# Seven shared PSUM banks with a cap per kind, two by-product tiles for the row maxima, transposes issued four in a run, and another plan

## The chip, the cores and the metric

The kernel runs on one core of a Trainium2 chip. The metric is the device time of one execution in microseconds (us); less is better. PE is the matrix engine (PEld its weight loads), DVE, ACT and POOL are the vector, scalar and general engines, SP issues most DMAs.

## What is computed

Two layers, each an attention block A and a feed-forward block B, on 2048 rows of 512 values, in float32:

```python
x = x + A(layernorm(x)); x = x + B(layernorm(x))      # twice, same weights
# A: 32 heads of 16, four segments of 512 rows, in order
logits = qs @ ks.T * scale + mask
a_dot = softmax(logits) @ vs
a_mem = (phi(qs) @ M) / (phi(qs) @ z + 1e-6)          # memory of the earlier segments
o = g * a_mem + (1 - g) * a_dot
M += phi(ks).T @ vs;  z += sum(phi(ks))
# B, with F = 1792
(silu(x @ w_gate) * (x @ w_up)) @ w_down
```

The mask takes away the keys that lie after the query.

## The kernel before

Precision. A float32 operand is split into a rounded part and a rest (two `float32r` halves); a product is three matmuls (high by high, low by high, high by low). `mm3` (L293), `qk_proj` (L469), `up` (L771) and `down` (L793) do this with 512-column matmuls. Some work stays in plain float32: the transposes by the identity (`ln_transpose` L378, `fin` L555, `post` L640, `mem_update` L677), the product of probabilities and values (`pv` L609), and the reading and updating of the memory (L657, L677). The text calls the first kind split matmuls and the second f32 matmuls.

Units. A unit `u` is 4 heads of one segment: 64 units in all, 8 to a segment (PER), 32 to a layer. For each unit:
- `mx_units` (L528) fills PSUM with the logits, queries on the partitions, 12 tiles of up to 512 columns (16 matmuls of 256, 256, 384 and 512 columns per head). DVE takes the row maximum of each piece (L548), writing the masked logits to a tile `junk` that nobody reads and the maximum to `mx`. `fin` transposes the maxima (L557), ACT negates them and sends them by DMA into a row of `cq`, the unit's query tile.
- `at_units` (L567) computes the logits again, keys on the partitions (L589), now with the maximum subtracted by that row; ACT takes the exponential (L595), POOL clears the masked triangle (L603), `pv` multiplies by the values (L618), and `post` normalises (DVE).

Around the units lie the projections (L290), the memory update (`mem_update`: four transposes of phi(k), an ACT copy, 16 small matmuls), and the feed-forward block of segment `j` (`ffn_items` L750), whose split matmuls are spread over the units of the segment after. In the first 8 to 10 units there is no feed-forward work to put between the attention's; after the last unit there is only feed-forward work left.

What sets the order. Nothing is ordered by hand. Every instruction is recorded as an `Op` with a cost, a priority and its buffers; `Program.issue` (L147) then plays the engines forward by a list of costs (LAT, DRAIN, TABLE and the costs at each `pe`, `act`, `dve`, `gp`), and takes at each moment, on the engine that is free first, the ready instruction with the lowest priority number. That order is written out, each engine runs its own in order, and semaphores keep the data right. The priority is the unit's number plus an offset from the tables ALONE, MIXED, EARLY, FFN and PRE. A change of these numbers moves instructions, not work.

PSUM. Of the 8 banks, `pj` has three that the planner hands out as they come free (projections, feed-forward, most transposes). `pmx` has two in a fixed alternation (row maxima), `plt` two in a fixed alternation (logits for the exponential), `ppv` one. A tile can be written only when the reader of the tile before it in the same bank is done.

Of the kernel before, what the change touches and what calls it, by code (L numbers as in the profile page):

```python
# [27 lines left out]
WOT = ("pmx_0", "pmx_1", "pj", "pj")  # L28
ALONE = {'at': (0.488, 0.659), 'lf': (-1.156, -0.458), 'mr': (1.485, 0.781), 'mu': (0.526, -0.286), 'qk': (-0.342, 0.72), 'v': (-0.297, -0.631), 'lp': (0.497, 0.642), 'mx': (-0.73, 0.16)}
MIXED = {'at': (0.319, 0.977), 'lf': (-0.896, 0.182), 'mr': (0.757, 0.781), 'mu': (0.246, 0.122), 'wo': (0.094, 1.841), 'qk': (-0.29, 0.416), 'v': (0.109, 0.348), 'lp': (0.111, 0.187), 'mx': (0.776, 0.745)}  # L30
EARLY = {'v': 1.068, 'qk': 0.531, 'o': 0.6}
FFN = {'ln': 2.081, 'up': 2.482, 'step': 1.143, 'second': 0.743, 'down': 0.177, 'gu': -0.061, 'd': 0.014}
LEAD = 1.0
PRE = {'c': -1.92, 'mb': 0.123, 'gate': -0.719, 'v': -1.763, 'dv': 0.124, 'qk1': -1.331, 'mx': -1.0}
NP = NF
TABLE = 1.28
TABLE_PRIO = 0.15
DRAIN = {("full", "cols"): 0.195, ("cols", "full"): 0.095}
# [3 lines left out]
    pe=dict(pe=0.01, act=0.35, dve=0.35, sp=0.34),  # L42
    act=dict(act=0.22, dve=0.28, pe=0.42, pool=0.35, sp=0.3),
    dve=dict(dve=0.13, act=0.28, pe=0.4, pool=0.31, sp=0.27),
    pool=dict(pool=0.1, dve=0.21, pe=0.28, act=0.25, sp=0.2),
    sp=dict(act=1.35, dve=1.35, pe=1.35, pool=1.35, sp=1.2),
)


class Buf:  # L50
    def __init__(self, prog, pool, tag, shape, dtype):
# [24 lines left out]
class Program:  # L76
# [70 lines left out]
    def issue(self):  # L147
# [16 lines left out]
        held = {tag: [] for tag in self.shared}  # L164
        for o in self.ops:
            if o.wait == 0:
                heapq.heappush(fut[o.eng], (o.ready, o.index, o))
        done, bus, table, mode = 0, 0.0, "exp", "full"
        while done < len(self.ops):
            best = None  # L170
            for e in engs:
                f, n = fut[e], now[e]
                while True:
# [31 lines left out]
            o = n[0][2]  # L205
            if e == "act" and o.table and o.table != table:
# [31 lines left out]
            for b in o.bufs:  # L238
                b.left -= 1
                if b.left == 0 and b.slot is not None:  # L240
                    free[b.tag].append((end + 0.25, b.slot))
                    for w in held[b.tag]:
                        w.ready = max(w.ready, end + 0.25)
# [10 lines left out]
def infini_swiglu(ctx: ExitStack, tc: tile.TileContext, x, wq, wk, wv, wo, beta, wg, wu, wd, out,  # L254
# [8 lines left out]
    P = Program({"pj": 3})  # L263
# [5 lines left out]
    def bank(tag, ring=1):  # L269
        return P.buf(psum, tag, [128, 512], F32, ring)  # L270

    def pe(n, passes, fn, reads, writes, loads=1, mode="full"):
        o = op("pe", max(passes * n / 2400 + 0.0025 + 0.0145 * loads * (passes == 1), 0.11 * loads), fn, reads, writes)
        o.mode = mode
        return o
# [4 lines left out]
    def dve(n, fn, reads, writes, fast=1):  # L280
        op("dve", n / 960 / fast + 0.0687, fn, reads, writes)
# [77 lines left out]
    def ln_norm(xt, view, xk, tags, on_act=False):  # L359
# [4 lines left out]
        gp(0.46, lambda: nc.gpsimd.tensor_tensor(out=rs.ap[:, 0:1], in0=mv.ap[:, 1:2], in1=mhalf.ap, op=OP.pow),  # L364
# [13 lines left out]
    def ln_transpose(xn, xh, xl, t, tag="pj"):  # L378
        ps = bank(tag)
        for kc in range(KC):  # L380
            pe(128, 2, lambda kc=kc: nc.tensor.transpose(ps.ap[:, kc * 128:(kc + 1) * 128],  # L381
                                                         xn.ap[:, kc * 128:(kc + 1) * 128], ident.ap),
               [xn, ident], [(ps, kc)])
# [5 lines left out]
    def split(raw, rv, hi, hk, hv, lo, lk, lv, on_pool=False):  # L389
        act(512, lambda: nc.scalar.copy(hv(hi.ap), rv(raw.ap)), [raw], [(hi, hk)], sbuf=True)  # L390
        if on_pool:
            gp(1.31, lambda: nc.gpsimd.tensor_sub(lv(lo.ap), rv(raw.ap), hv(hi.ap).bitcast(F32)),  # L392
# [76 lines left out]
    def qk_proj(G, n, nm, tag="pj", nt="nat", rt="raw"):  # L469
# [12 lines left out]
        gp(0.62, lambda: nc.gpsimd.tensor_scalar(out=nat.ap[:, 0, :], in0=raw.ap, scalar1=1.0, scalar2=0.0,  # L482
# [456 lines left out]
```

## Time and profile before

| | |
|---|---|
| time, median of 3 runs (lowest, highest) | 1980.16 us (1979.6, 1980.47) |
| the profiled execution's own time | 1978.77 us |
| its span, first to last instruction | 1977.0 us |
| mean granted PE clock | 0.995 |
| PE busy, PEld busy | 1922.9 us (97%), 1488.2 us (75%) |
| ACT busy, POOL busy | 1171.0 us (59%), 997.2 us (50%) |

A matmul's record runs from its start to a modelled end that lies well after the start of the next, so that records overlap. Idle time of PE in the profile is therefore less than the time lost: a stretch in which the next matmul starts late shows as busy until the record before it ends. The distance between starts is what counts.

### The profile page before, as it was taken

What the parts mean: (1) busy time and instruction counts of PE and PEld (TensorE: products, weight loads), DVE (VectorE), ACT (ScalarE), POOL (GpSimd) and SP (SyncE); (2) the same over time, 40 slices, a digit from 0 to 9 for tenths busy, and PEclk for the clock granted to TensorE, in tenths of its full rate; (3) what the DMA queues carried; (4) which work ended last, traced back from release to release, by engine and by line L of the source; (5) the groups of instructions that cost most, each with busy time, mean ns of one, the idle gap of its engine ahead of it and who ended that gap; (6) DMA issues with size and microseconds to landing.
All of it is one profiled execution on the core that took longest, in us unless ns stands there. A gap on an engine that the chain in (4) does not pass through costs nothing.

```text
span 1977.0 us, 33401 instructions
## 1 busy us (share of the span) xinstructions
PE 1922.9 (97%) x11136; PEld 1488.2 (75%) x11136; DVE 1173.9 (59%) x3376; ACT 1171.0 (59%) x2268; POOL 997.2 (50%) x1139
## 2 busy tenths in 40 slices
PE   7998999999999999999999999999999999999998
PEld 5675777777777777777777787777777777777786
DVE  4775664656656565555645675555755557654454
ACT  3565576656666566655766756666565665664332
POOL 6455555465554555454654655546554464445100
PEclk9999999999999999999999999999999999999999
DMA  7544544456434554444644546434554355333332
GB/s 223 162 134 139 152 120 120 113 142 190 128 107 118 145 182 134 118 123 145 183 138 120 134 145 169 137 101 140 150 159 129 97 155 159 109 87 113 110 96 75
DMA packets 250490, 266.98 MB, mean 135 GB/s; under 512 B 17872, under 2 KB 166352, under 8 KB 250320
## 3 DMA queue, kind: packets, MB, share of 16 engines
q1 hardware_dynamic: 248272, 264.33, 46.3%
q8 instruction: 89, 1.46, 0.3%
q10 hardware_dynamic: 2048, 0.53, 0.1%
q14 instruction: 81, 0.66, 0.1%
HBM read 197.15 MB, written 67.11 MB: 134 GB/s over the span
## 4 chain that ended last, share of the span: by engine, by line
PE 85%; DVE 6%; issue 3%; DMA 3%; ACT 2%; POOL 1%; SPq 0%; DVEq 0%; ACTq 0%; POOLq 0%
PE pj L779 28%; PE pj L290 16%; PE pj L802 13%; PE pmx L541 8%; PE plt L589 7%; PE ppv L618 7%; DVE junk L548 2%; PE pmx L802 2%; PE pj L665 1%; PE pj L381 1%; DMA ck<-scrk 1%; ACT p L595 0%; DVE r L630 0%; PE pj L557 0%; PE pj L681 0%
## 5 line engine op out<-in xcount | busy, mean ns | idle before, releaser
L548 DVE CUSTOM_DVE_ANT_0 junk<-pmx,amask 128x128 bf16<-128x128 f32 (+3 forms) x1024 | 497.6, 486 | 252.0 <-PE pmx L541 200.6
L779 PE MATMUL pj<-fh,gu 128*128 128x512 f32 x1568 | 524.7, 399 | 1.3 <-ACT sg L786 0.7
L595 ACT ACTIVATE p<-plt 128x512 f32<-128x512 f32 (+2 forms) x768 | 334.8, 458 | 175.7 <-PE plt L589 148.5
L802 PE MATMUL pj<-d,h 128*128 128x512 f32 x1176 | 361.6, 399 | 5.8 <-DVE fl L386 1.6
L392 POOL TENSOR_TENSOR gu<-rw,gu 128x512 fp32r<-128x512 f32 x196 | 257.3, 1315 | 208.4 <-ACT gu L390 191.2
L779 PEld LDWEIGHTS pj<-fh,gu 128*128 128x128 f32 x1568 | 289.2, 188 | 55.5 <-ACT sg L786 1.4
L541 PE MATMUL pmx<-ck,cq 127*128 127x256 f32 x992 | 287.6, 337 | 14.5 <-DVE mx L548 10.1
L779 PE MATMUL pj<-fl,gu 128*128 128x512 f32 x784 | 301.5, 401 | 0.0
L589 PE MATMUL plt<-cq,ck 128*128 128x512 f32 x992 | 283.8, 333 | 4.3 <-ACT p L595 2.3
L802 PEld LDWEIGHTS pj<-d,h 128*128 128x128 f32 x1176 | 217.3, 188 | 58.1 <-DVE fl L386 2.3
L541 PEld LDWEIGHTS pmx<-ck,cq 127*128 127x128 f32 x992 | 180.4, 190 | 64.2 <-DVE mx L548 14.5
L589 PEld LDWEIGHTS plt<-cq,ck 128*128 128x128 f32 x992 | 182.8, 190 | 39.2 <-ACT p L595 8.6
L390 ACT CAST gu<-rw 128x512 fp32r<-128x512 f32 x226 | 139.3, 620 | 121.8 <-PE pj L779 64.2
L603 POOL TENSOR_SCALAR_AFFINE_SELECT p<-p 128x512 f32<-128x512 f32 x192 | 124.5, 648 | 170.8 <-ACT p L595 170.0
L805 DVE TENSOR_TENSOR fx<-fx,pj 128x512 f32<-128x512 f32 x196 | 133.1, 682 | 93.0 <-PE pj L802 92.2
L779 PEld LDWEIGHTS pj<-fl,gu 128*128 128x128 f32 x784 | 147.2, 188 | 29.3 <-issue 1.0
L392 POOL TENSOR_TENSOR d<-rw,d 128x512 fp32r<-128x512 f32 x98 | 125.8, 1301 | 61.4 <-ACT d L390 36.8
L787 DVE TENSOR_TENSOR sg<-sg,pj 128x512 f32<-128x512 f32 x112 | 76.6, 684 | 99.5 <-PE pj L779 59.3
L618 PE MATMUL ppv<-p,vt 128*32 128x512 f32 (+2 forms) x1536 | 135.2, 454 | 0.0
L628 DVE STREAM_TRANSPOSE tt<-ppv 128x512 f32<-128x512 f32 x64 | 45.8, 716 | 117.8 <-PE ppv L618 117.7
L786 ACT ACT_TABLE_LOAD x87 | 111.6, 1283 | 2.8 <-PE pj L779 1.3
L790 DVE TENSOR_TENSOR h<-sg,h 128x512 fp32r<-128x512 f32 x112 | 94.6, 845 | 27.7 <-ACT h L789 27.2
(165 smaller groups left out, 3218.3 us busy)
## 6 DMA issues: line engine op xcount, KB each, us to landing
rw<-in_B_w_gate_dram SPq DMA_DIRECT2D x112, 256.0 KB, 3.1
rw<-in_B_w_down_dram SPq DMA_DIRECT2D x112, 256.0 KB, 2.7
rw<-in_B_w_up_dram SPq DMA_DIRECT2D x112, 256.0 KB, 3.0
cq<-scrq SPq DMA_DIRECT2D x124, 192.0 KB, 3.2
ck<-scrk SPq DMA_DIRECT2D x124, 192.0 KB, 4.3
scrq<-nat SPq DMA_DIRECT2D x31, 512.0 KB, 2.8
scrk<-nat SPq DMA_DIRECT2D x30, 512.0 KB, 2.7
rw<-in_A_wv_dram SPq DMA_DIRECT2D x32, 256.0 KB, 2.8
```

Source lines behind the costliest of these rows:

```text
L290: pe(n, passes, lambda: nc.tensor.matmul(view(ps.ap), lhsT=av(a.ap), rhs=bv(b.ap), start=start, stop=stop), [(a, rk[0]), (b, rk[1])], [ps])
L390: act(512, lambda: nc.scalar.copy(hv(hi.ap), rv(raw.ap)), [raw], [(hi, hk)], sbuf=True)
L392: gp(1.31, lambda: nc.gpsimd.tensor_sub(lv(lo.ap), rv(raw.ap), hv(hi.ap).bitcast(F32)), [raw, (hi, hk)], [(lo, lk)])
L541: nc.tensor.matmul(ps.ap[:, a * 256:a * 256 + nk], lhsT=cq.ap[0:127, 2 * j + p, qt * 128:(qt + 1) * 128], rhs=ck.ap[0:127, p, 0:nk], start ...
L548: dve(w, lambda a=a, qt=qt, w=w, ps=ps, junk=junk: nc.vector.tensor_tensor_reduce(out=junk.ap[:, :w], in0=ps.ap[:, a * 256:a * 256 + w], i ...
L589: nc.tensor.matmul(ps.ap[:, c0:c0 + n_], lhsT=ck.ap[:, p, k0:k0 + 128], rhs=cq.ap[:, 2 * j + p, 512 - n_:512], start=True, stop=True)
L595: act(w, lambda Pb=Pb, o0=o0, w=w, i0=i0: nc.scalar.activation(Pb.ap[:, idx, o0:o0 + w], ps.ap[:, i0:i0 + w], AF.Exp, scale=SCALE), [ps], ...
L603: gp(0.593, lambda: nc.gpsimd.affine_select(out=v(), in_=v(), pattern=[[0, 4], [1, 128]], compare_op=OP.is_ge, fill=0.0, base=0, channel_m ...
L618: nc.tensor.matmul(ps.ap[32 * i:32 * i + 32, q0:q0 + w], lhsT=vt.ap[:, kt, VW * hd:VW * hd + 32], rhs=f_[sl].ap[:, idx, c0:c0 + w], start= ...
L779: pe(512, 1, lambda x=x, y=y, kc=kc, z=z, ps=ps, wt=wt: nc.tensor.matmul(ps.ap, lhsT=wt.ap[:, x, kc], rhs=T[y].ap[:, :, kc], start=(z == 0 ...
L802: pe(512, 1, lambda x=x, y=y, z=z, ps=ps, ht=ht, wt=wt, cs=cs: nc.tensor.matmul(ps.ap, lhsT=ht.ap[:, y, cs], rhs=wt.ap[:, x, :], start=(z ...
L805: dve(512, lambda ps=ps, t=t: nc.vector.tensor_add(X.ap[:, t, :], X.ap[:, t, :], ps.ap), [ps, (X, t)], [(X, t)])
```

## The change

- PSUM. `pj`, `pmx` and `plt` become one set of seven banks, `ps`, given out as they come free; `ppv` stays. At most 3 of the seven may hold row-maximum tiles, 3 logits, 4 the rest (CAP).
- Transposes. The four transposes of a tile (layer norm, phi(k), memory) and the two matmuls that fill one bank of a memory read are recorded as one operation, so that nothing comes between them. All f32 matmuls are marked as one mode; where the planner would change the mode, it first takes ready work of the mode it is in, up to 0.572 units later in priority (MODE_PRIO). For activation tables the like allowance goes from 0.15 to 2.787.
- `junk` has two tiles in turn, `nm` one in place of two.
- The planner's costs and latencies, and all tables of offsets, have other values. The units' early table holds two units longer, and the third copy of the query and key tiles one unit longer.

No arithmetic is added or left out; the number of matmuls, reductions, exponentials and splits is the same (a few instructions change engine).

```diff
-WOT = ("pmx_0", "pmx_1", "pj", "pj")
-ALONE = {'at': (0.488, 0.659), 'lf': (-1.156, -0.458), ...
+WOT = ("pmx", "pmx", "pj", "pj")
+ALONE = {'wo': (-0.72, 3.126), 'at': (-2.429, -2.271), ...
-FFN = {'ln': 2.081, 'up': 2.482, 'step': 1.143, 'second': 0.743, 'down': 0.177, 'gu': -0.061, 'd': 0.014}
+FFN = {'ln': 1.126, 'up': 2.673, 'step': 1.087, 'second': 0.857, 'down': 0.247, 'gu': -0.315, 'd': 2.454}
-TABLE_PRIO = 0.15
-DRAIN = {("full", "cols"): 0.195, ("cols", "full"): 0.095}
+TABLE_PRIO = 2.787
+DRAIN = {("full", "f32"): 0.09, ("f32", "full"): 0.0}
+MODE_PRIO = 0.572
+CAP = {"pmx": 3, "plt": 3, "pj": 4}
+SLACK = 0.103
...
-                            if not free[b.tag]:
+                            if not free[b.tag] or used[b.kind] >= CAP[b.kind]:
...
+            if e == "pe" and o.mode != mode:
+                stay = [x for x in n if x[2].mode == mode and x[0] < o.prio + MODE_PRIO
+                        and (x[2].need is None or x[2].need.slot is not None
+                             or (used[x[2].need.kind] < CAP[x[2].need.kind]
+                                 and any(y[0] <= start + 1e-9 for y in free[x[2].need.tag])))]
+                if stay:
+                    x = min(stay)
...
-    P = Program({"pj": 3})
+    P = Program({"ps": 7})
...
-        for kc in range(KC):
-            pe(128, 2, lambda kc=kc: nc.tensor.transpose(ps.ap[:, kc * 128:(kc + 1) * 128],
-                                                         xn.ap[:, kc * 128:(kc + 1) * 128], ident.ap),
-               [xn, ident], [(ps, kc)])
+        def turn():
+            for kc in range(KC):
+                nc.tensor.transpose(ps.ap[:, kc * 128:(kc + 1) * 128], xn.ap[:, kc * 128:(kc + 1) * 128], ident.ap)
+        pe(512, 2, turn, [xn, ident], [ps], mode="f32", cost=0.435)
...
-                    ps = bank("pmx", ring=2)
+                    ps = bank("pmx")
-                        junk = sb("junk", [128, 512], BF16)
+                        junk = sb("junk", [128, 512], BF16, ring=2)
...
-                ps = bank(f"pmx_{t % 2}") if end else bank("pj")
+                ps = bank("pmx" if end and t % 2 else "pj")
```

Three places in the order of PE's instructions. The numbers behind a name are its bank or copy and the buffer. Line numbers differ between the two kernels: L541/L563 fills row-maximum tiles, L557/L579 is the transpose of the maxima, L290/L312 a projection, L681/L709 the transposes of phi(k), L720 the memory update, L618/L640 `pv`, L802/L829 `down`.

First place: PE, early, the row-maximum tiles at the end of unit 0 and the start of unit 1. Before:

```order
L541 MATMUL pmx_0_544<-ck0_99,cq0_67 128x512
L541 MATMUL pmx_1_553<-ck0_99,cq0_67 128x256 x2
L541 MATMUL pmx_0_562<-ck0_99,cq0_67 128x384
L541 MATMUL pmx_1_570<-ck0_99,cq0_67 128x512
L541 MATMUL pmx_0_575<-ck1_215,cq1_204 128x256 x2
L541 MATMUL pmx_1_583<-ck1_215,cq1_204 128x384
L557 MATMUL pj_2_587<-ident_65,mx_0_483 16x128
```

and now:

```order
L563 MATMUL ps_1_538<-ck0_99,cq0_67 128x512
L312 MATMUL ps_5_513<-xl_186,wq_354 128x512 x2
L563 MATMUL ps_2_550<-ck0_99,cq0_67 128x256 x2
L563 MATMUL ps_3_562<-ck0_99,cq0_67 128x384
L563 MATMUL ps_4_565<-ck0_99,cq0_67 128x512
L563 MATMUL ps_6_577<-ck1_234,cq1_212 128x256 x2
L579 MATMUL ps_0_580<-ident_65,mx_0_450 16x128
```

Before, six tiles in a row go to two banks in turn, so that every tile waits for the reader of the tile two ahead of it; now each goes to another bank.

Second place: PE, in the middle of the program (second layer, its first segment), the transposes of phi(k) around a `pv`. Before:

```order
L618 MATMUL ppv_11909<-p1_11789,vt0_82 32x128 x4
L802 MATMUL pj_0_11892<-d_1_11588,h_0_11695 128x512
L802 MATMUL pj_2_11906<-d_1_11588,h_0_11695 128x512
L681 MATMUL pj_1_11936<-ident_65,phik_0_10566 128x128
L802 MATMUL pj_2_11906<-d_0_11581,h_2_11515 128x512
L681 MATMUL pj_1_11936<-ident_65,phik_0_10566 128x128
L802 MATMUL pj_2_11906<-d_1_11588,h_0_11695 128x512
L681 MATMUL pj_1_11936<-ident_65,phik_0_10566 128x128
L802 MATMUL pj_2_11906<-d_0_11581,h_2_11515 128x512
L681 MATMUL pj_1_11936<-ident_65,phik_0_10566 128x128
```

and now:

```order
L579 MATMUL ps_1_11916<-ident_65,mx_1_11631 16x128
L709 MATMUL ps_0_11918<-ident_65,phik_0_10801 128x128 x4
L640 MATMUL ppv_11927<-p0_11661,vt0_82 32x512 x4
L640 MATMUL ppv_11927<-p1_11706,vt0_82 32x384 x4
L640 MATMUL ppv_11927<-pc_11758,vt0_82 32x256 x4
L640 MATMUL ppv_11927<-p1_11706,vt0_82 32x128 x4
L720 MATMUL ps_3_11949<-vt0_82,of_11945 32x34 x16
```

The four transposes stood one by one between split matmuls; now they stand together, and with the transpose of the maxima, `pv` and the memory update make one run of f32 matmuls.

Third place: PE, near the last of the program, `down` of the last feed-forward block. Before:

```order
L802 MATMUL pmx_1_22092<-d_0_22074,h_2_22045 128x512
L802 MATMUL pmx_0_22086<-d_1_22079,h_0_22101 128x512
L802 MATMUL pmx_1_22092<-d_1_22079,h_0_22101 128x512
L802 MATMUL pmx_0_22117<-d_0_22074,h_2_22045 128x512
L802 MATMUL pmx_0_22117<-d_1_22079,h_0_22101 128x512
```

and now:

```order
L829 MATMUL ps_1_22102<-d_0_22067,h_2_22041 128x512
L829 MATMUL ps_2_22100<-d_1_22073,h_0_22097 128x512
L829 MATMUL ps_1_22102<-d_1_22073,h_0_22097 128x512
L829 MATMUL ps_3_22114<-d_0_22067,h_2_22041 128x512
L829 MATMUL ps_6_22117<-d_0_22067,h_2_22041 128x512
```

The third result tile went to the bank of the first (`pmx_0`), one matmul after that was complete; now it goes to another bank.

Counted over all of PE's rows: the 9632 matmuls are the same in both. Stretches of f32 matmuls with no split matmul between them are 385 before and 119 now. On ACT, loads of an activation table are 174 before and 152 now.

More of the change, by code (lines that the diff above doesn't have):

```diff
@@ L267, in sb, with bank, pe @@
         return P.buf(pool, tag, shape, dtype, ring)
[L269 to L273, printed above, removed]
+    def bank(kind):
+        if kind == "ppv":
+            return P.buf(psum, kind, [128, 512], F32)
+        return Buf(P, psum, "ps", [128, 512], F32, kind)
+    def pe(n, passes, fn, reads, writes, loads=1, mode="full", cost=None):
+        o = op("pe", cost or max(n / 2400 + 0.018 * loads, 0.109 * loads), fn, reads, writes)
         o.mode = mode
@@ L581, in f @@
                         f_[sl] = sb("pc", [128, 4, 256])
-                ps = bank("plt", ring=2)
+                ps = bank("plt")
                 need = [(cq, j), (cq, "m"), (ck, 0), (ck, 1)]
@@ L620, in go @@
                                          rhs=f_[sl].ap[:, idx, c0:c0 + w], start=(x == 0), stop=(x == 3))
-            pe(1280, 4, go, [(vt, e) for e in range(8)] + [f_[0], f_[1], f_[2]], [ps], mode="cols")
+            pe(1280, 4, go, [(vt, e) for e in range(8)] + [f_[0], f_[1], f_[2]], [ps], mode="f32", cost=2.29)
         def post():
@@ L640, in post, with turn @@
                     m, tp = g["mem"], bank("pj")
-                    for t in range(4):
-                        o = pe(128, 2, lambda t=t: nc.tensor.transpose(tp.ap[:, t * 128:(t + 1) * 128],
-                                                                       m.ap[:, t], ident.ap), [m, ident], [(tp, t)])
-                        o.deps |= set(f_["pv"].ops[:1])
+                    def turn():
+                        for t in range(4):
+                            nc.tensor.transpose(tp.ap[:, t * 128:(t + 1) * 128], m.ap[:, t], ident.ap)
+                    pe(512, 2, turn, [m, ident], [tp], mode="f32", cost=0.435).deps |= set(f_["pv"].ops[:1])
                 dve(512, lambda: nc.vector.transpose(of.ap, Y.ap.rearrange("p a b -> p (a b)")), [Y], [of])
@@ L679, in mem_update, with turn @@
         vt, ps, phi = VT[G % 2], bank("pj"), g["phik"]
-        for t in range(4):
-            pe(128, 2, lambda t=t: nc.tensor.transpose(ps.ap[:, t * 128:(t + 1) * 128],
-                                                       phi.ap[:, t * 128:(t + 1) * 128], ident.ap),
-               [phi, ident], [(ps, t)])
+        def turn():
+            for t in range(4):
+                nc.tensor.transpose(ps.ap[:, t * 128:(t + 1) * 128], phi.ap[:, t * 128:(t + 1) * 128], ident.ap)
+        pe(512, 2, turn, [phi, ident], [ps], mode="f32", cost=0.435)
         pk = sb("of", [128, 512])
@@ L694, in go @@
                                      rhs=vt.ap[:, t, hd:hd + 2 * VW], start=(t == 0), stop=(t == 3))
-        pe(2 * VW * 4, 4, go, [pk] + [(vt, c) for c in range(8)], [pm], loads=3, mode="cols")
+        pe(2 * VW * 4, 4, go, [pk] + [(vt, c) for c in range(8)], [pm], mode="f32", cost=0.39)
         tmp, m = sb("mtmp", [128, 2, VW]), Mb[n]
@@ L833, in infini_swiglu @@
     for t in range(4):
-        ln_fin(0, t, ("pmx_0", "pmx_1", "pj", "ppv")[t])
+        ln_fin(0, t, ("pmx", "pmx", "pj", "ppv")[t])
     XTL = xT[0][0]
```

72 lines of the change are left out of this document (42 added, 30 removed).

## The prediction, made before the run

> **What bounds the kernel.** I read the engines' shares first, then four stretches of the program, then PE's waits, then single stretches of PE.
>
> ```profile
> span 1977.0 us, 33401 instructions
> PE 1922.9 (97%) x11136; PEld 1488.2 (75%) x11136; DVE 1173.9 (59%) x3376; ACT 1171.0 (59%) x2268; POOL 997.2 (50%) x1139
> PE 85%; DVE 6%; issue 3%; DMA 3%; ACT 2%; POOL 1%; SPq 0%; DVEq 0%; ACTq 0%; POOLq 0%
> ...
> 0.00:25.00 25.00, 12.52 (x48) 10.31 (x49) 14.20 (x46) 12.11 (x21) 16.18 (x35) 0.93 0.57 179
> 25.00:200.00 175.00, 160.71 (x1066) 112.63 (x1065) 112.79 (x399) 96.19 (x233) 96.60 (x120) 0.96 0.55 162
> 200.00:1850.00 1650.00, 1629.83 (x9518) 1270.30 (x9517) 981.31 (x2833) 1024.40 (x1949) 884.43 (x985) 1.00 0.47 135
> 1850.00:1977.00 127.00, 119.82 (x509) 94.92 (x508) 65.60 (x99) 38.33 (x66) 0.00 (x0) 0.99 0.31 92
> ```
>
> (The stretches' columns: length, busy time of PE, PEld, DVE, ACT, POOL, granted PE clock, DMA share, GB/s.) PE is the bound. The change neither adds nor removes a matmul, so it can win only what PE loses between them. Idle is 12.5 us before 25, 14.3 to 200, 20.2 to 1850, 7.2 at the end: 54 us. The loss is larger, because a record outlives its turn:
>
> ```profile
> 703.23 2.48 PE L802 MATMUL pj<-d,h 128*128 128x512 f32 x10
> ```
>
> Ten 512-column matmuls, each of a 0.40 us record, take 2.48, so one starts every (2.48 - 0.40) / 9 = 0.231 us, and a late start hides its first 0.17 us behind the record before it. How this looks early on:
>
> ```profile
> 59.03 0.94 PE L541 MATMUL pmx<-ck,cq 127*128 127x256 f32 x3
> 59.39 0.08 DVE L548 DVE_READ_ACCUMULATOR2_ANT mx<- 128x1 f32 x1
> 59.52 0.19 PEld L541 LDWEIGHTS pmx<-ck,cq 127*128 127x128 f32 x1 [0.30 <-DVE mx L548]
> 60.30 0.08 DVE L548 DVE_READ_ACCUMULATOR2_ANT mx<- 128x1 f32 x1
> 60.53 0.47 PE L541 MATMUL pmx<-ck,cq 127*128 127x512 f32 x1 [0.56 <-DVE mx L548]
> ...
> PEld pmx L541 <- DVE mx L548: 8.8, 21, 0.8
> PEld plt L589 <- ACT p L595: 6.2, 14, 0.9
> PE pmx L541 <- DVE mx L548: 7.1, 16, 1.3
> ```
>
> Four fills stand one behind the other, and from 59.03 to 60.53 PE does what needs about 0.6 us; each fill starts as DVE finishes the tile two ahead. The three waits are those of 25 to 200 (total, times, longest). So the early loss is for two banks, not for an engine: DVE is busy 113 of those 175 us.
>
> **The banks.** The first place in the order shows six fills on two banks; now seven banks take turns. I priced every PE row (0.231 us for 512 columns, by width below that, f32 matmuls by their own rows) and summed PE's work between a tile's last matmul and the first of the next tile in its bank. What a bank needs in between: 0.17 for the last record's end, the reader, and about 0.07 for the signal (DVE ends at 59.47, the load starts at 59.52; elsewhere up to 0.15). The readers:
>
> ```profile
> L548 DVE CUSTOM_DVE_ANT_0 junk<-pmx,amask 128x512 bf16<-128x512 f32 x256 | 175.5, 686 | 81.6 <-PE pmx L541 71.4
> L548 DVE CUSTOM_DVE_ANT_0 junk<-pmx,amask 128x256 bf16<-128x256 f32 x256 | 107.4, 420 | 6.3 <-DVE mx L548 0.2
> L548 DVE DVE_READ_ACCUMULATOR2_ANT mx<- 128x1 f32 x1024 | 84.1, 82 | 0.2
> L548 DVE CUSTOM_DVE_ANT_0 junk<-pmx,amask 128x128 bf16<-128x128 f32 x256 | 73.0, 285 | 110.4 <-PE pmx L541 96.9
> L595 ACT ACTIVATE p<-plt 128x512 f32<-128x512 f32 x256 | 147.1, 600 | 78.8 <-PE plt L589 62.2 <-PE ppv L618 15.5
> ```
>
> A row-maximum tile needs 0.17 + 0.686 + 0.082 + 0.07 = 1.0 us at 512 columns and 1.1 for the pair of small pieces; logits need 0.84. In the first 190 us of PE work (some 230 us of time) 87 of 359 reuses come after less than 1.0 us of work before, and 7 of 369 now. The shortfalls add to 24.7 us before and 1.2 now; in all the rest to 8.6 before and nothing now. So the waits for banks cost about 33 us, and can give between 0 (if the reader's queue, not the bank, is the limit) and 33. I take 18 early and 5 later, **23**, nearer the upper end: 72% and 58% of the shortfall, since PE packed closer meets the other engines sooner.
>
> **The clock.** Within the early stretch the granted clock falls where PE idles:
>
> ```profile
> 50.00:75.00 25.00, 20.96 (x88) 14.91 (x92) 19.62 (x75) 11.72 (x29) 15.42 (x16) 0.93 0.45 144
> 150.00:175.00 25.00, 21.35 (x154) 12.87 (x154) 12.66 (x38) 16.44 (x39) 14.93 (x20) 0.86 0.44 124
> ```
>
> The stretch of 25 to 200 has 0.96: 0.04 x 175 = 7 us of full clock lost; the two quoted pieces are 1.75 and 3.5 of it. Their idle time should shrink with the bank waits. Between 0 and 7 I take **4**. The Trainium skill ("TensorE: Matmul & The Clock Gate", section "A second HAM failure mode: psum-queue depth-cycling") says that short idles of PE between groups that cycle through banks make the clock gate swing; by that rule the whole 7 would come back. Here 75 to 150 has a clock of 1.00 with bank waits in it, which speaks against the whole.
>
> **Transposes in a run, f32 matmuls in a run.** The second place in the order, in the trace of before:
>
> ```profile
> 700.42 0.60 PE L381 MATMUL pj<-ident,xn 128*128 128x128 f32 x4
> ...
> 1015.09 1.32 PE L802 MATMUL pj<-d,h 128*128 128x512 f32 x5
> 1016.34 1.71 PE L618 MATMUL ppv<-p,vt 128*32 128x512 f32 x16
> 1018.30 0.40 PE L618 MATMUL ppv<-p,vt 128*32 128x128 f32 x8
> 1018.63 0.74 PE L802 MATMUL pj<-d,h 128*128 128x512 f32 x2
> 1019.21 0.27 PE L681 MATMUL pj<-ident,phik 128*128 128x128 f32 x1
> 1019.56 0.27 PE L681 MATMUL pj<-ident,phik 128*128 128x128 f32 x1
> 1020.59 0.40 PE L290 MATMUL pj<-wvh,xh 128*128 128x512 f32 x1
> ```
>
> Four transposes with a split matmul behind each take 1020.59 - 1019.21 = 1.38 us; four split matmuls are 0.92, so a transpose alone costs 0.114. In a run it costs (0.60 - 0.27) / 3 = 0.109. So four in a run save 0.02 us a tile: **nothing**. `pv` is another matter: it starts 0.33 us after the last of the five before it (0.10 over 0.231), and the second matmul behind it 0.34 after the first (0.11 over): some 0.2 us to go there and back. A neighbour that joins it can save up to 0.1. Of 64 `pv`, 40 stood alone and 6 do now, and of 24 memory updates 21 and 4: 51 joins at most, between 0 and 5 us; I take **4**. If every one of the 266 stretches that vanish saved 0.09, it would be 24; the rows above say no for a transpose.
>
> **What costs or gives nothing.** Loads of an activation table, 174 to 152, at
>
> ```profile
> L786 ACT ACT_TABLE_LOAD x87 | 111.6, 1283 | 2.8 <-PE pj L779 1.3
> L548 DVEq EVENT_SEMAPHORE  x630: 21/21/21, 43.3 to 1776.6; - x158
> ```
>
> 1.28 us are 28 us of ACT, which is busy 59%; they hide beside PE, and without that cover only those ahead of a wait of PE would count. The second `junk` drops a wait of DVE on itself, at most 630 x 0.021 = 13 us of DVE, hidden likewise but for the early row maxima, where it is in the 18. One `nm` for two: its next use is a unit away (20 us), far beyond the DMA that reads it.
>
> **Both ends.**
>
> ```profile
> 9.05 1.97 PE L381 MATMUL pmx<-ident,xn 128*128 128x128 f32 x8 [9.05 <-ACT xn L370]
> ...
> 1966.98 2.59 PE L802 MATMUL pmx<-d,h 128*128 128x512 f32 x10 [1.50 <-ACT h L789]
> 1970.11 3.03 PE L802 MATMUL pmx<-d,h 128*128 128x512 f32 x12 [0.54 <-DVE p L805]
> ```
>
> At the start SP now sends the rows of x ahead of a piece of `wv`, whose issue took the first 0.4 us, and ACT no longer casts that piece between: about 1 us. At the end, by the third place in the order, the wait of 0.54 (0.7 between starts) goes, that of 1.50 for `h` stays, and the last two additions now come due 0.23 us apart in place of 0.7, so that the second waits 0.4 more. Together I take **2**, between -1 and 4.
>
> **New waits.** The planner now counts about 0.27 us from ACT or DVE to PE (0.17 or 0.16 plus SLACK), 0.42 and 0.40 before, so it places matmuls sooner behind what they need. A weight tile `gu` is loaded, cast by ACT and completed by POOL before PE may use it; of 223 reuses of its three copies 1 lay under 3 us of PE work before, 13 do now. The row of PE's waits that shows it before:
>
> ```profile
> PE pj L779 <- ACT gu L390: 0.9, 1, 0.9
> ```
>
> One wait in the whole program. I take **-1**, nearest to that row; the bound is the second rival. Behind such a matmul everything on PE queues.
>
> **The sum.** 23 + 4 + 4 + 2 - 1 = 32 us off the profiled execution's own 1978.8 (span 1977.0 and 1.8 around it), which lies 1.4 below the median: 1946.8 there, **1948** against the median.
>
> **The rivals.**
> - DVE and ACT take the banks' place: PE early waits for row maxima and exponentials, whatever bank they sit in. For it: DVE's row maxima of a unit are 16 x (0.486 + 0.082), some 9 us, as long as PE's own attention work for it; against it: DVE's 113 of 175. Half the bank and clock terms are left, 13 of 27: 1962.
> - Weights late, **slower**: ACT serves `gu` behind exponentials, since its offset moved from -0.061 to -0.315 (later). The price is a wait at each of 224 pieces; at 0.2 us it is 45, which gives 1993. It decides from 33 / 224 = 0.15 us a piece. Against it: one wait in the row above, and 204 of the reuses leave over 4 us for a cast of 0.6 and a subtraction of 1.3.
> - A stretch of f32 matmuls costs 0.09 to leave and the joins bring 24 in place of 4: 1928.
> - The change does not do what it says: caps of 3 and 3 with 4 others on 7 banks only move the waits to the other kinds: 1978.
> - Long runs of transposes lose the clock. The first 25 us hold a run of 16 transposes at a clock of 0.93, 1.75 us lost; some twelve stretches now hold 12 or more transposes: 12 x 1.75 = 21, which gives 1969. The Trainium skill (the same page, section "Part 4: PE-mode transpose") says that transposes do not count as activity for the gate. From 200 to 1850 the clock reads 1.00 with 35 runs of four in the program, so the trace gives no sign of it.
>
> **Chances.** The forecast 0.62 (its own range 1932 to 1960), DVE and ACT 0.17, the joins 0.06, no effect 0.04, late weights 0.07, the clock 0.04. A measurement of this kernel can tell some 0.2%, 4 us. Faster: 0.62 + 0.17 + 0.06 + 0.04 = 0.89; same 0.04; slower 0.07. The range takes in the whole shortfall and half the joins (33 + 7 + 12 + 4 = 56 off) at its lower end, and at the upper a fifth of the bank term and nothing from clock and joins (5 + 2 - 1 = 6 off): 1924 to 1974.
>
> **What would show it.** Right: from 25 to 200 PE's waits for DVE `mx` and ACT `p` fall from 22 us to under 8, DVE is busier there, the clock reads 0.98 or more; 200 to 1850 gets shorter by some 10; a run of four transposes still costs 0.109 each. Wrong: a new large row of PE waiting for ACT `gu`, or for `lt`'s row of maxima; a `pv` whose surroundings got no cheaper; an early stretch as long as before.

## The result and the profile after

| | before | changed |
|---|---|---|
| time, median (lowest to highest) | 1980.32 us (1979.6 to 1984.02) | 1923.14 us (1921.63 to 1923.6) |
| the profiled execution's own time, its span | 1978.77, 1977.0 us | 1923.43, 1921.7 us |

The ratio is 0.9706, with a 95% interval of 0.9689 to 0.9723: 57 us less, where 32 were forecast. The time lies 0.9 us under the low end of the range. The page of the changed kernel (engines, then the shares of the chain that ended last) and its four stretches, cut as in the prediction:

```profile
span 1921.7 us, 33511 instructions
PE 1883.9 (98%) x11136; PEld 1497.5 (78%) x11136; DVE 1158.1 (60%) x3376; ACT 1134.6 (59%) x2246; POOL 998.1 (52%) x1139
PE 91%; DVE 4%; DMA 2%; issue 1%; ACT 1%; POOL 1%; SPq 0%; DVEq 0%; POOLq 0%; ACTq 0%
...
0.00:25.00 25.00, 15.51 (x66) 12.56 (x67) 16.60 (x49) 13.54 (x23) 17.89 (x38) 1.00 0.57 184
25.00:200.00 175.00, 160.45 (x1177) 121.97 (x1176) 121.50 (x452) 98.83 (x249) 106.69 (x137) 0.98 0.64 181
200.00:1850.00 1650.00, 1641.86 (x9616) 1310.38 (x9615) 983.73 (x2823) 1001.78 (x1940) 873.48 (x965) 1.00 0.47 136
1850.00:1921.70 71.70, 66.03 (x283) 52.57 (x281) 36.28 (x56) 20.40 (x35) 0.00 (x0) 0.99 0.26 81
```

The chain of work is PE's for 91% of the span, 85% before. From 25 to 200 PE is no busier than before (160.45 and 160.71), yet it begins 1177 matmuls there, 1066 before. Records overlap, so busy time hides what was won, and I measure a **loss** instead: the time at which a matmul begins, less the work of all matmuls ahead of it at the prediction's prices (0.231 us for 512 columns and so on, 1856 us in all for both kernels). **Early** is the loss over the first 190 us of that work, **late** the rest:

| loss, us | at 5 us of work | early | late | together |
|---|---|---|---|---|
| before | 16.1 | 58.7 | 58.2 | 116.9 |
| changed | 11.3 | 37.6 | 23.2 | 60.8 |

The early part gives 21 us, close to the prediction (18 for banks, 4 for the clock, 1 at the start), but partly by luck: 4.8 of the 21 are the start, and putting the old banks back costs only 12 early (e5 below). The late part gives 35, where the prediction had about 9. PE's waits (total, times, longest) from 25 to 200, PE and then its weight loads, the larger ones that involve row maxima or exponentials, and the longest:

```profile
PE ps L563 <- DMA ck<-scrk: 5.8, 1, 5.8
PE ps L611 <- DVE mx L570: 1.2, 1, 1.2
PE ps L579 <- DVE mx L570: 1.2, 1, 1.2
PE ps L611 <- ACT p L617: 0.8, 1, 0.8
...
PEld ps L611 <- ACT p L617: 1.7, 3, 1.1
PEld ps L579 <- DVE mx L570: 1.4, 1, 1.4
PEld ps L563 <- DVE mx L570: 0.5, 1, 0.5
```

The three rows of before had 22.1 us (8.8, 6.2 and 7.1); of them, fills behind DVE's maxima or ACT's exponentials, 3.0 are left (0.8, 1.7, 0.5). The row of L611 behind `mx` (1.2) is a new kind: a logits tile waits for the reader of a row-maximum tile, whose bank it takes over. The longest wait is now one for data, the first copy of the keys.

### The profile page after: what moved, and what is told of

Read it like the earlier page. It is cut to its first block, busy times and chain, and to the rows that moved or that the text cites. A ratio compares the mean times of both kernels' runs of the same rounds, so it can differ in the third digit from the quotient of the medians.

```text
span 1921.7 us, 33511 instructions
## 1 busy us (share of the span) xinstructions
PE 1883.9 (98%) x11136; PEld 1497.5 (78%) x11136; DVE 1158.1 (60%) x3376; ACT 1134.6 (59%) x2246; POOL 998.1 (52%) x1139
## 4 chain that ended last, share of the span: by engine, by line
PE 91%; DVE 4%; DMA 2%; issue 1%; ACT 1%; POOL 1%; SPq 0%; DVEq 0%; POOLq 0%; ACTq 0%
PE ps L806 31%; PE ps L312 17%; PE ps L829 16%; PE ps L563 8%; PE ps L611 8%; PE ppv L640 7%; PE ps L690 1%; PE ps L404 1%; DVE junk L570 1%; DVE Y L654 1%; DMA ck<-scrk 1%; PE ps L709 0%; DMA cq<-nm 0%; PE ps L579 0%; PE ps L720 0%
## 5 line engine op out<-in xcount | busy, mean ns | idle before, releaser
L570 DVE CUSTOM_DVE_ANT_0 junk<-ps,amask 128x128 bf16<-128x128 f32 (+3 forms) x1024 | 462.3, 486 | 247.9 <-PE ps L563 245.3
L806 PE MATMUL ps<-fh,gu 128*128 128x512 f32 x1568 | 524.2, 396 | 1.2 <-DVE fl L408 1.2
L617 ACT ACTIVATE p<-ps 128x512 f32<-128x512 f32 (+2 forms) x768 | 321.1, 469 | 165.1 <-PE ps L611 158.6
L829 PE MATMUL ps<-d,h 128*128 128x512 f32 x1344 | 393.7, 395 | 1.0 <-ACT h L816 1.0
L806 PEld LDWEIGHTS ps<-fh,gu 128*128 128x128 f32 x1568 | 291.1, 188 | 57.0 <-DVE fl L408 1.4
L829 PEld LDWEIGHTS ps<-d,h 128*128 128x128 f32 x1344 | 252.0, 188 | 59.3 <-ACT h L816 1.5
L806 PE MATMUL ps<-fl,gu 128*128 128x512 f32 x784 | 297.6, 396 | 0.0
L563 PE MATMUL ps<-ck,cq 127*128 127x256 f32 x976 | 270.4, 331 | 11.2 <-DMA ck<-scrk 5.8
L611 PE MATMUL ps<-cq,ck 128*128 128x512 f32 x976 | 257.6, 324 | 5.8 <-DMA cq<-nm 3.1
L563 PEld LDWEIGHTS ps<-ck,cq 127*128 127x128 f32 x976 | 180.1, 190 | 43.3 <-issue 10.8
L611 PEld LDWEIGHTS ps<-cq,ck 128*128 128x128 f32 x976 | 180.0, 188 | 37.2 <-DVE r L652 1.7
L806 PEld LDWEIGHTS ps<-fl,gu 128*128 128x128 f32 x784 | 147.5, 188 | 31.2 <-issue 0.4
L414 POOL TENSOR_TENSOR d<-rw,d 128x512 fp32r<-128x512 f32 x98 | 125.6, 1295 | 41.2 <-ACT d L412 38.4
L640 PE MATMUL ppv<-p,vt 128*32 128x512 f32 (+2 forms) x1536 | 135.3, 454 | 0.0
L617 ACT ACT_TABLE_LOAD x75 | 96.2, 1283 | 20.0 <-PE ps L611 18.6
```

Of the source, the lines that this page charges most:

```text
L414: gp(1.25, lambda: nc.gpsimd.tensor_sub(lv(lo.ap), rv(raw.ap), hv(hi.ap).bitcast(F32)), [raw, (hi, hk)], [(lo, lk)])
L563: nc.tensor.matmul(ps.ap[:, a * 256:a * 256 + nk], lhsT=cq.ap[0:127, 2 * j + p, qt * 128:(qt + 1) * 128], rhs=ck.ap[0:127, p, 0:nk], start ...
L570: dve(w, lambda a=a, qt=qt, w=w, ps=ps, junk=junk: nc.vector.tensor_tensor_reduce(out=junk.ap[:, :w], in0=ps.ap[:, a * 256:a * 256 + w], i ...
L611: nc.tensor.matmul(ps.ap[:, c0:c0 + n_], lhsT=ck.ap[:, p, k0:k0 + 128], rhs=cq.ap[:, 2 * j + p, 512 - n_:512], start=True, stop=True)
L617: act(w, lambda Pb=Pb, o0=o0, w=w, i0=i0: nc.scalar.activation(Pb.ap[:, idx, o0:o0 + w], ps.ap[:, i0:i0 + w], AF.Exp, scale=SCALE), [ps], ...
L640: nc.tensor.matmul(ps.ap[32 * i:32 * i + 32, q0:q0 + w], lhsT=vt.ap[:, kt, VW * hd:VW * hd + 32], rhs=f_[sl].ap[:, idx, c0:c0 + w], start= ...
```

## The experiments

All runs but two, with the loss of their profiled execution; e17 and e18 repeat the changed kernel and e16 and stand at the end. Where two kernels have the same early order, their early losses differ by up to 5 us (before and e13: 58.7 and 63.2), so less than that is not read from one profile. The kernel before had a median of 1980.1 to 1981.5 us in the five sets of runs.

| run | median us | ratio to before, 95% | early | late |
|---|---|---|---|---|
| e1, before with seven banks, order kept | 1979.71 | 0.9994 [0.9979, 1.001] | 59.7 | 61.0 |
| e2, before with four shared of seven, order kept | 1982.34 | 1.0007 [0.9993, 1.002] | 61.5 | 58.4 |
| e3, changed, transposes apart | 1924.97 | 0.9719 [0.9695, 0.9742] | 38.6 | 21.4 |
| e4, changed, f32 operations apart | 1929.45 | 0.9742 [0.9719, 0.9765] | 40.4 | 26.9 |
| e5, changed, old banks, new plan | 1970.02 | 0.9949 [0.9935, 0.9964] | 49.3 | 56.1 |
| e6, changed, old latencies | 1941.96 | 0.9815 [0.9797, 0.9834] | 63.1 | 17.8 |
| e7, changed, old offsets | 1957.42 | 0.9896 [0.9876, 0.9916] | 44.0 | 50.5 |
| e8, before, new offsets and latencies | 2019.07 | 1.0203 [1.0183, 1.0223] | 58.2 | 99.9 |
| e9, changed, last freed bank first, order kept | 1945.92 | 0.9821 [0.9807, 0.9836] | 45.3 | 38.4 |
| e10, before, seven banks, new plan | 1994.33 | 1.0065 [1.005, 1.008] | 85.0 | 47.2 |
| e11, changed, no grouping | 1941.3 | 0.9799 [0.9784, 0.9813] | 39.0 | 39.9 |
| e12, changed, old banks and old offsets | 1974.33 | 0.9967 [0.9954, 0.9979] | 54.3 | 58.1 |
| e13, before, no table loads | 1973.41 | 0.9971 [0.9956, 0.9987] | 63.2 | 48.5 |
| e14, e1 without table loads | 1957.81 | 0.9885 [0.987, 0.99] | 57.1 | 39.2 |
| e15, changed, no table loads | 1921.7 | 0.9703 [0.9689, 0.9718] | 35.4 | 21.5 |
| e16, changed, latencies by part | 1918.37 | 0.9688 [0.9673, 0.9702] | 35.7 | 19.2 |

### Seven banks in the old order

The kernel before, each engine's order kept to the row; only the bank of a tile is another (e1). In e2 the same is done with the four banks of `pmx` and `plt` alone.

```diff
-                    tag = b.tag if b.slot is None else f"{b.tag}_{b.slot}"
+        banks = list(range(7))
+        for o in order:
...
+                        alive[b] = [banks.pop(0), len(b.ops)]
+                        tag = f"ps_{alive[b][0]}"
...
+                        banks.append(alive.pop(b)[0])
```

> The kernel before, every engine's order unchanged; only the bank of each row-maximum, logits and other tile is another: one of seven, the one that has been free longest. Nothing else of the change is in it. Theory A (PE waited for banks, also later in the program, where the reader of a bank stands in its engine's queue): the early part gets some 14 us shorter and the rest some 14 us shorter, about 1952. Rival B (later in the program it is the planner's new costs and tables that took the waits away, banks matter early alone): about 1965. Rival C (it is the joined f32 stretches): no more than 15 off, nothing of it after the first 230 us.

> As the first, but only the four banks of row maxima and logits are dealt together (the one free longest), the three others stay as they were. Theory A: the short reuses early fall only from 87 to 73, so 4 to 8 us off, about 1974, and the rest of the program, where the three banks are the short ones, hardly moves. If the fixed alternation of two and two were the trouble and not the number of banks: 15 or more off.

Neither gained anything, though in e1 the reuses of a bank under 1.0 us of work fell from 87 to 16 early and from 40 to 15 late. Theories A and B for e1 and both forecasts for e2 fall: the banks alone are worth nothing in the old order. Only rival C for e1 (no more than 15) was met; its cause, the joined f32 stretches, is tried next and comes to about 8. e1's waits from 25 to 200, then from 200 to 1850:

```profile
PE ps L571 <- DVE mx L562: 5.8, 3, 3.0
PE ps L555 <- DMA ck<-scrk: 3.1, 2, 1.9
PE ps L707 <- ACT of L699: 2.4, 2, 2.1
PE ps L603 <- DVE mx L562: 1.9, 3, 1.2
PE ps L555 <- DVE mx L562: 1.5, 5, 0.5
...
PE ps L555 <- ACT sg L800: 6.8, 10, 2.0
PEld ps L555 <- ACT sg L800: 13.5, 18, 2.1
```

Early, the fills' wait for the maxima (L555; 7.1 before) is nearly gone, and PE stands at operations that want data instead: the transpose of the maxima (L571) and the memory update (L707). A logits tile (L603) now also waits for the reader of a row-maximum tile. Late there is a row that the kernel before did not have among its larger ones: a row-maximum tile waits for ACT's silu (`sg`), since it now takes over the bank of a gate tile. The longest of them, PE and ACT (start, length):

```profile
476.59 0.46 PE L707 MATMUL ps<-vt,of 128*32 128x34 f32 x32
479.03 0.50 PE L555 MATMUL ps<-ck,cq 127*128 127x512 f32 x1 [1.98 <-ACT sg L800]
...
475.40 0.62 ACT L404 CAST wk<-rw 128x512 fp32r<-128x512 f32 x1 [4.32 <-DMA rw<-in_A_wk_dram]
475.93 1.14 ACT L404 CAST gu<-rw 128x512 fp32r<-128x512 f32 x2
477.09 1.28 ACT L800 ACT_TABLE_LOAD   x1
478.38 0.60 ACT L800 ACTIVATE sg<-ps 128x512 f32<-128x512 f32 x1
479.00 1.28 ACT L609 ACT_TABLE_LOAD   x1
```

The gate tile's reader stood behind three casts and a table load, and PE for 1.98 us behind it. That is a second limit, which the separate banks of before had kept away from the row maxima.

### Transposes apart, f32 operations apart

The changed order and banks; in e3 the second to fourth transpose of a tile each go behind the next split matmul (119 stretches of f32 matmuls become 236), in e4 neighbouring f32 operations are put apart in the same way (207 stretches).

```diff
+            if o.mode == "full" and late:
+                emit(*late.pop(0))
```

> The changed kernel, order and banks unchanged but for one thing: of the four transposes of a tile, each but the first is put behind the next split matmul (where nothing needs it sooner). Stretches of f32 matmuls rise from 119 to 236, with pv and its neighbours as they were. If a transpose costs 0.11 us wherever it stands, as the rows of before say: plus 0 to 2 us, 1923 to 1925. If every stretch costs 0.09 to leave: plus 10, 1934.

> The changed kernel, banks unchanged, but wherever two f32 operations stand next to each other on PE, the second waits until a split matmul has been put between (unless something needs it sooner): memory updates, memory reads, transposes of maxima and pv stand apart more often, transposes of one tile stay together; 207 stretches in place of 119. If going to pv or a memory update and back costs 0.2 us and a neighbour saves half of it: 88 stretches times 0.1, plus 9 us, 1932. If joins are worth what I said of them in the sum (51 joins, 4 us): plus 4 to 7. If joins are worth nothing: 1923.

Transposes: 1.8 us for 117 more stretches, 0.02 each at most, since the intervals of e3 and the changed kernel overlap. Whole operations: 6.3 us for 88 stretches, 0.07 each; the intervals of the ratios just overlap, the times of the runs do not (1929.07 at the lowest, 1923.6 at the highest). The rows of the prediction had said nothing for a transpose and up to 0.1 for a neighbour of `pv`. In the changed kernel:

```profile
947.37 0.60 PE L404 MATMUL ps<-ident,xn 128*128 128x128 f32 x4
947.80 0.27 PE L579 MATMUL ps<-ident,mx 128*16 128x128 f32 x1
948.01 1.71 PE L640 MATMUL ppv<-p,vt 128*32 128x512 f32 x16
```

A run of four still takes (0.60 - 0.27) / 3 = 0.109 us each.

### One part of the change undone, planned anew

e5 has the old banks (three, two and two, each kind's given out as they come free), e6 the old latencies and costs, e7 the old offset tables, e11 no grouping of modes; all else is the change.

```diff
-    P = Program({"ps": 7})
+    P = Program({"pj": 3, "pmx": 2, "plt": 2})         # e5
-        gone = end + LAT[e]["pe"]
+        gone = end + 0.25                              # e6, with the old LAT and costs
-ALONE = {'wo': (-0.72, 3.126), ...
+ALONE = {'wo': (0.094, 1.841), 'at': (0.488, 0.659), ...   # e7, and the other tables
-MODE_PRIO = 0.572
+MODE_PRIO = 0.0                                        # e11
```

> The changed kernel with the banks of before (three handed out, two and two in turn), planned anew; new latencies, new offset tables, transposes in one operation, modes grouped. What is open: seven banks in the old order gave nothing (ratio 0.9994), so the gain of 57 us lies in the new order. Theory C, the planner can only make the better order with seven banks to deal: 1960 or more (over 35 of the 57 us lost). Theory L, the refitted latencies make it, or theory T, the new offsets do, whatever the banks: 1923 to 1935. By bank reuses under 1.0 us of PE work (77 early and 43 late here, 87 and 40 before, 7 and 0 in the changed kernel) the sum of the prediction would give 1923 + 23 = 1946.

> The changed kernel with the planner's latencies and costs of before (LAT, the 0.25 us to free a bank, the costs of PE and POOL work), planned anew; all else new. Theory L: over 35 of the 57 us are lost, 1958 or more. Theories C and T: under 10 lost, 1921 to 1933.

> The changed kernel with the offset tables of before (ALONE, MIXED, EARLY, FFN, PRE and the allowance for activation tables), planned anew; seven banks, new latencies, modes grouped. Theory T: over 35 of the 57 us are lost, 1958 or more. Theories C and L: under 10 lost, 1921 to 1933. If this and the kernels with the old banks and the old latencies all lose 15 to 30, no part carries it alone (theory S, the parts add up).

> The changed kernel without the grouping of modes (an allowance of 0 instead of 0.572), planned anew; transposes are still four in one operation. 276 stretches of f32 matmuls instead of 119. Theory G, grouping is worth what it was at fixed order (88 more stretches cost 6.3 us, so 157 more cost 11): 1931 to 1938. Theory G2, grouping also makes the plan's orders better, as the 49 us between the new offsets with old banks without it (2019) and with it and runs of four (1970) suggest: 1950 or more.

Against the changed kernel's 1923.1 the old banks cost 47 us, the old offsets 34, the old latencies 19, no grouping 18. The four add to 118, twice the gain, so **the gain can't be divided into shares of the parts**: what one is worth depends on the others. Each number is one plan; what an arbitrary change of the fitted numbers costs was not tried, so part of each loss may be that of leaving a plan fitted as a whole. The caps, the second `junk` and the longer early tables were not undone by themselves. e5 alone met the bound for the theory that the banks are needed (1960 or more), e7 missed the one for offsets (1958) by 0.6 us, and e6 and e11 fell between the values that were expected. The places differ: latencies count early (25 of loss) and are 5 better late in their old form; grouping (17) and offsets (27) count late; old banks cost 12 early and 33 late. e6's waits from 25 to 200:

```profile
PE ps L610 <- DMA cq<-nm: 7.9, 3, 3.6
PE ps L610 <- DMA fx<-nm: 4.9, 3, 3.6
PE ps L562 <- DMA ck<-scrk: 4.8, 1, 4.8
```

PE waits 12.8 us for rows of maxima (`fx` is the buffer of the third query tile), 2.4 in the changed kernel.

### Parts alone

e8 is the kernel before with the new offsets and latencies; e10 with seven banks, planned anew; e12 is the change with old banks and old offsets, so the kernel before with grouping, transposes in a run and new latencies.

```diff
-    P = Program({"pj": 3})
+    P = Program({"ps": 7})                             # e10, with CAP
-ALONE = {'at': (0.488, 0.659), ...
+ALONE = {'wo': (-0.72, 3.126), ...                     # e8, with the new LAT
```

> The kernel before with the new offset tables and the new latencies, but its old banks, its transposes one by one and no grouping of modes. Theory T or L (alone or together): 1925 to 1945. Theory C: 1970 to 1985. Theory S: 1945 to 1970.

> The kernel before with seven banks in one set, caps of 3, 3 and 4, and planned anew with its old latencies and offsets, transposes one by one, no grouping of modes. Without the banks the changed kernel loses 47 us. If the banks' freedom in the plan is what the gain comes from, by itself: 1930 to 1945. If it only pays together with offsets fitted to it (the old offsets cost the changed kernel 34) or with the grouping: 1960 to 1985.

> The changed kernel with both the old banks and the old offsets: that is the kernel before plus transposes in one operation, grouping of modes, new latencies, two junk tiles. Stretches of f32 matmuls 194 instead of 385. At 0.07 us a stretch that goes: 13 off the kernel before, 1967. If offsets and banks belong together (theory P, pairs), it is faster than old banks with new offsets (1970): 1945 to 1965. If each part brings its own (theory S): 1970 + 34 = 2004, slower than before.

e8 and e10 are slower than before, by 38 and 13 us, beyond what was expected of either; e12 brings 7, and none of the three values expected of it came.

With grouping, runs of transposes and new latencies in place, four kernels differ in banks and offsets alone: both old 1974 (e12), new offsets 1970 (e5), seven banks 1957 (e7), both new 1923. So the new offsets bring 4 us on the old banks and 34 on seven; seven banks bring 17 with the old offsets and 47 with the new. Of the 51 us, 30 come only from the two together. e8 lacks the grouping and the runs besides the banks: with them the same offsets and latencies on the old banks take 49 us less (e5), so e8 does not show that the new offsets are bad for the old banks. e10 from 25 to 200:

```profile
25.00:200.00 175.00, 142.46 (x899) 108.02 (x898) 93.25 (x332) 83.43 (x200) 89.80 (x107) 0.87 0.50 147
...
PE ps L565 <- DVE mx L556: 19.6, 7, 5.8
PE ps L597 <- DMA fx<-nm: 5.7, 1, 5.7
```

In this plan PE's queue stands up to 5.8 us at a transpose of maxima (L565) that DVE has not finished, and the granted clock reads 0.87 (0.96 before). Seven banks with the old offsets do better than the kernel before once the latencies are new and modes are grouped (e7), so the old offsets alone are not to blame; which of the other two mends it was not tried.

### The new order on banks soon used again

The changed kernel with every engine's order kept; the planner deals the bank that came free last instead of the first.

```diff
-                fr = min(free[b.tag])
+                fr = max((y for y in free[b.tag] if y[0] <= start + 1e-9), default=min(free[b.tag]))
```

> The changed kernel with the order of every engine kept to the row; only which bank a tile gets is changed, the bank that came free last instead of the one that came free first. Reuses of a bank under 1.0 us of PE work: 48 early and 3 late (7 and 0 in the changed kernel), late ones under 1.3 us: 303 (52). Old banks cost 47 us when the order was planned anew on them. Theory C1, the chip gains from the longer time between two uses of a bank: by the prediction's pricing a shortfall of 23 us, so 1935 to 1948. Theory C2, seven banks matter only in the plan, which may open tiles earlier, and the chip doesn't need the longer time: 1921 to 1929.

22.8 us more, inside what theory C1 said. So in the new order the kernel needs the time between two uses of a bank; in the old order (e1) more of it bought nothing. Waits for the maxima, from 25 to 200 and from 200 to 1850:

```profile
PE ps L563 <- DVE mx L570: 8.3, 14, 1.5
...
PE ps L563 <- DVE mx L570: 3.4, 6, 1.3
PE ps L806 <- DVE mx L570: 2.6, 9, 0.4
PEld ps L806 <- DVE mx L570: 6.5, 9, 0.8
```

The total came out as the shortfall under 1.0 us gives it (23), but not the place: the shortfall is 21.9 early and 1.1 late, the loss grew by 7.7 early and 15.2 late. Late, the first row is no larger than in the changed kernel (3.7); new is that gate and up tiles of the feed-forward block (L806) wait for the reader of a row-maximum tile. There 303 reuses lie under 1.3 us in place of 52. A reader that is free at once needs 1.0; that in the middle of the program it is often in other work, so that 1.0 to 1.3 does not do, is what the counts suggest, and no row shows it by itself.

### ACT's table loads

Relu in place of Silu, order and banks kept, so that all but one of the table loads go: before (e13), e1 (e14), changed (e15). The feed-forward block gives another result.

```diff
-nc.scalar.activation(sg.ap, pg.ap, AF.Silu)
+nc.scalar.activation(sg.ap, pg.ap, AF.Relu)
```

> The kernel before, order and banks unchanged, with Relu in place of Silu in the feed-forward block, so that ACT loads no activation table there (174 loads of 1.28 us become 1): the feed-forward result is another one. ACT loses 222 us of work that stand in its queue ahead of what PE waits for. Theory Q (ACT's queue is a second limit beside the banks, and either alone gives little): 1970 to 1979. Rival (ACT's loads alone are what the old order loses): 1940 to 1955. Rival (ACT's loads always hide): 1979 to 1983.

> The kernel with seven banks in the old order (e1: 1979.7), again with Relu in place of Silu and no table loads, so another feed-forward result. There PE's new waits were for banks that ACT's silu (20 us, 28 times) or DVE's row maxima had still to read. Theory Q: with ACT's queue short the seven banks now bring what they bring in the new order (about 22): 1950 to 1962, at least 12 under the kernel with the old banks and no table loads. Rival (the old order waits for DVE or for data, not for ACT): within 5 us of that kernel.

> The changed kernel, order and banks unchanged, with Relu in place of Silu and no table loads (another feed-forward result). If the loads hide beside PE in the new order, as the prediction has it: 1919 to 1924. If they still stand in PE's way: 1905 to 1917.

e13 and e14 came as theory Q expected, e15 as the prediction had it. Without loads the old order gains 7 us on its old banks and 22 on seven banks; seven banks then bring 15.6 (1973.41 to 1957.81), where with the loads they brought nothing. In the changed kernel the loads cost 1.4, within the intervals, and the changed kernel run again (e17, 1921.41) leaves nothing of it. e1 and then e14, from 200 to 1850, with e14's wait for silu:

```profile
200.00:1850.00 1650.00, 1626.02 (x9499) 1269.47 (x9498) 979.01 (x2834) 1024.80 (x1944) 887.27 (x988) 1.00 0.47 135
200.00:1850.00 1650.00, 1638.51 (x9590) 1287.04 (x9589) 987.73 (x2846) 809.41 (x1787) 885.12 (x984) 1.00 0.47 136
...
PE ps L555 <- ACT sg L800: 0.6, 1, 0.6
```

ACT loses 215 us of work (1024.80 to 809.41), and PE's wait of 6.8 us falls to 0.6. The late loss goes from 61.0 to 39.2; the early one, where the feed-forward block hardly runs, stays.

### Early and late by themselves

New latencies and costs up to 230 us of planned time, the old ones after that (e16); then, side by side on one chip, the changed kernel (e17) and this one (e18) again.

```diff
+            late = start >= LATE          # 230.0
+            lat = LAT2 if late else LAT
```

> The changed kernel planned with the new latencies and costs up to 230 us of planned time and with the old ones after that. With the old ones throughout, the loss in the first 190 us of PE work was 63.1 (37.6 with the new) and behind it 17.8 (23.2). If the two parts are independent: 37.6 + 17.8 = 55.4 in place of 60.8, so 1918. If not, or if chance in the plan makes the 5 us: 1921 to 1930.

> The changed kernel itself, on the same chip as the kernel with latencies by part, so that the 5 us between them are compared side by side: 1922 to 1924.

> The kernel with new latencies to 230 us of planned time and old ones after, beside the changed kernel. If the early and the late part are independent and the old latencies serve the late part better: 3 to 7 us under the changed kernel. If it was chance between chips: within 2 us of it.

Side by side: 1921.41 us (1921.3 to 1922.9) and **1916.3 us** (1915.29 to 1917.89), ratios to before of 0.9702 [0.9687, 0.9718] and 0.9679 [0.9663, 0.9694]. The runs do not overlap, and the 5.1 us are the 5 that e6's late loss had promised, as two independent parts would have it; this is the fastest version of all. Why larger latencies suit the late part was not tried.

## Why the prediction was wrong

Its direction was right and its range 0.9 us too high. The step that failed is the pricing of the late part: 5 us for banks, taken from shortfalls in the old order, and nothing for the new offsets. Undone, they cost 33 and 27 us late (e5, e7), and 35 us came where about 9 stood. The early total was right partly because its errors cancelled. Step by step:

- **"The banks", 23.** That e9 loses 22.8 us, close to the 23, is luck: in the old order, on which the 23 was worked out, seven banks gave nothing (e1), and the places are others. What failed is "I take 18 early and 5 later": early, the banks are worth 8 at a fixed order and 12 when planned anew, late 15 and 33 (e9, e5). The prediction took the reader to be free at once, and counted 1.0 us as enough.
- **"What costs or gives nothing", the table loads.** They do hide in the new order (e15). In the old order they were the limit that stood right behind the banks: 22 us once the banks were free (e14 against e1). The prediction priced the banks as if their readers were free, and set the loads at nothing because they hide beside PE; it did not ask what the reader of a freed bank has in its queue. The late part, undersized by 26 us, takes banks, the places of the loads and the f32 stretches together. How its 35 us divide between them can't be said, since undone one by one the parts add to more than the whole.
- **The plan.** Nothing in the sum stood for the new offsets by themselves. They are worth 4 us on the old banks (e5 against e12) and 34 on seven (e7). New latencies were priced at -1 for new waits; no row of PE waiting for `gu` came, so the rival of late weights fell. The latencies were worth 19, all of it early.
- **Joins of f32 matmuls, 4.** Undersized: e4 and e3 give 6.3 and 1.8, about 8 at a fixed order for 205 of the 266 stretches. The price was near (0.08 a join taken, 0.07 a stretch measured), the count of 51 too small: e4 has 88. Grouping as a rule of the plan is worth 18 (e11); its 157 stretches at 0.07 are 11, so by this estimate some 7 come from the order that it makes. The rival of 24, which put 0.09 on every stretch, failed on transposes: those cost 0.02 or less (e3).
- **Transposes in a run, nothing.** Right (e3, and 0.109 us in the row above). The rival by which they lose the clock fell: the clock reads 1.00 from 0 to 25 and from 200 to 1850.
- **The clock, 4.** The number was near, 3.5 (0.96 to 0.98 over the 175 us from 25 to 200), but not by the bank waits. The rows of 25 to 200 in e5 (old banks, new plan) and e1 (seven banks, old order):

```profile
25.00:200.00 175.00, 159.41 (x1070) 114.44 (x1069) 109.87 (x417) 98.13 (x239) 98.53 (x122) 0.99 0.58 167
25.00:200.00 175.00, 156.05 (x1068) 112.66 (x1066) 111.29 (x394) 96.83 (x235) 97.12 (x119) 0.95 0.56 162
```

  The clock is 0.99 with the old banks and 0.95 with seven. It went with the latencies: 0.97 to 0.99 in every run that plans the early part with the new ones, 0.87 to 0.96 in every run with the old. In the first 25 us it rose from 0.93 to 1.00, but there e13 and e14, in the order of before, read 1.00 too and e1 0.86, so that is not put down to the change. The whole 7 did not come back. The 3.5 that are left lie here:

```profile
25.00:50.00 25.00, 19.23 (x111) 15.49 (x110) 8.31 (x29) 6.14 (x12) 14.33 (x18) 0.86 0.93 250
150.00:175.00 25.00, 21.33 (x127) 16.16 (x127) 17.36 (x66) 15.20 (x41) 17.49 (x22) 1.00 0.63 189
```

  0.14 x 25 = 3.5, in the piece with the wait of 5.8 for the keys, and 150 to 175, which read 0.86 before, is at 1.00.
- **Both ends, 2.** Undersized: the start gives 4.8 (16.1 to 11.3); the last 105 us of work lose 1.8 in place of 5.0, so 3 more. The start goes with the offsets: the loss at 5 us of work is 10.8 to 13.4 in all runs with the new ones and 16.1 to 18.0 in those with the old.
- **The rival "DVE and ACT take the banks' place"** is, in its kind, what e1 shows for the old order, though e1 gained nothing where the rival left half. In the changed kernel it did not come about; that the order around DVE and ACT was changed along with the banks is the likely reason. It had been taken for an alternative to the forecast; it was a condition of it.

## What to carry to other kernels

When an engine waits at two limits in turn, removing either alone seems to bring little: price a removed wait by what would be late next in the same place, and remove both in an experiment before calling either worthless. Priorities and buffers have to be fitted together: the new offsets bring 34 us on seven banks and 4 on the old ones, and a part of such a change tried alone can come out slower than doing nothing (1994 and 2019 here against 1981). A shared pool also couples its users: a tile then waits for the slowest reader of any kind, so look at who frees a bank, not only at how many there are.

## What was not expected of the hardware

- A table load on ACT takes 1.28 us and the next instruction starts 0.01 us behind it (477.09 + 1.28, then 478.38). The Trainium skill ("ScalarE: Activation LUTs", section "What ACT_TABLE_LOAD costs") gives the same 1283 ns and adds a drain of some 1380 ns for a switch; no such time shows in these rows.
- Taking turns through seven banks is no gain by itself: 0.9994 [0.9979, 1.001] in e1. The Trainium skill ("Perfetto Trace Analysis", section "Matmul Optimizations") says to use all eight banks. Both kernels use all eight; how seven of them are dealt mattered by 23 us in the new order (e9) and not in the old.
- Leaving and re-entering f32 matmuls costs about 0.07 us around `pv` or a memory update (e4) and 0.02 or less around a single 128 by 128 transpose (e3).
